# A third gate/value unit begun in the first batch, and batch 5's values loaded behind index 6's keys and queries

## The chip, the cores and the metric

One core of a Trainium2 chip runs the whole program. The metric is the device time of one execution in microseconds (us). Times named by "at" are counted from the start of the profiled span. Batches and banks are counted from 0, so batch 5 is the sixth.

## The reference

Attention without a softmax, followed by a gated feed-forward layer over all tokens:

```
attn = relu(q @ k.T / sqrt(64)) ** 2 / 448          # 8 batches, 12 heads, 448 tokens, 64 wide
x    = (attn @ v), heads side by side               # 3584 tokens x 768
out  = (relu(x @ w_gate) * (x @ w_val)) @ w_out     # 768 -> 1536 -> 768, float32
```

Inputs are float32 in memory and are cast to bfloat16 as they are loaded.

## The kernel before

**Work of a batch.** Scores are made in 21 tiles per batch: three quads of heads (two pairs of two) times seven groups of 64 tokens. `tile_of` makes one with four matmuls, each on a quarter of the array; `relu2` reads it out, ScalarE (ACT) through a Relu (L232) and VectorE (DVE) through a square (L233). `values` (L263) makes a quad of attention outputs with 28 matmuls from the tile `vn`, reads them out, and `exchange` (L258) copies them with the two halves of the partitions swapped, for the units below.

**Gate/value units.** `gv_unit` (L302) makes 128 columns of the hidden layer for one batch: 12 steps of four matmuls on the weights `gv`, into two neighbouring banks of PSUM, then `g_sb` (ACT, L320, reads the first bank) and the product into `hT` (DVE, L321, reads the second). A batch has 12 units. The two banks come from a taker made by `rotation`:

```
sc_first, sc_later, acc = rotation((0, 2, 4)), rotation((0, 2)), rotation((6, 4))
```

Scores and values after the first batch take from `sc_later`, units from `acc`. A take happens when a unit's first step runs. Two units of batch 0 have banks of their own, 4 and 2 (BEGUN_IN, L583): they are begun in `first_batch` (L609) with the four steps that need no exchange. Weight chunk c, loaded by `load_gv(c)`, serves units 2c and 2c+1.

**Order.** It is written out by hand. In iteration b (1 to 6) the loop at L760 runs the units of batch b-1 on TensorE and puts events between their steps: scores and values of the next batches, spread by `paced` (L739), and single events at (unit, step), such as loads. `step` and `turned` (L717 to L726) place the four pieces by which a later batch's keys and queries are turned: `regroup` (L176) on DVE copies them into `kr` or `qr`, and `transpose_grouped` (L183) turns them by DMA transposes issued on SP's queue into `kqT`. Every engine runs its instructions in the order of the program.

**Output stages.** After iterations 2, 4 and 6, `out_pair` (L355) multiplies two batches' hidden layers by `w_out`, in a Strassen form of seven products over four tiles of tokens. Its banks are fixed: P = (6, 7, 0, 1) and Q = (2, 3, 4, 5) for the four tiles. It opens with P's first tile and ends with the adds (L399) of Q's last two. The next iteration's first unit follows, or, after iteration 6, `gv_pair` with fixed banks of its own.

**Loads.** All of them are issued on POOL's queue by `dma_in` (L115). `hold(b)` (L687) puts two tiny copies on POOL that read the last of batch b's turned keys and queries, so POOL issues nothing behind them before those have landed. From batch 2 on all natural keys and queries share one pair of tiles, `kn` and `qn`; values have two tiles in turn. In iteration 4 the values of batch 5 are loaded at unit 0, step 4, and `hold(5)` with the load of index 6 comes at unit 5, step 4. The pieces for batch 5 stand at units 2 and 3, those for batch 6 at units 9 and 10. The first values of batch 5 are made at unit 11, step 5 (L778).

Of the kernel before, what the change touches and what calls it, by code (L numbers as in the profile page):

```python
# [16 lines left out]
def kernel(  # L17
# [172 lines left out]
    def rotation(numbers):  # L190

        turn = [0]

        def take():
            n = numbers[turn[0] % len(numbers)]
            turn[0] += 1
            return banks[:, n:n + 2, :]
        return take
# [52 lines left out]
    def value_passes(b, qd, ps, i0, i1):  # L251

        attn, v_sb = attn_of(b, qd), v_b[b % NB]
        for i in range(i0, i1):
            mm4([ps[:, r, :S] for r in range(2)], lambda r, c: v_sb[:, 2 * qd + c, i, :],
                lambda r, c: attn[:, 2 * i + c, :], i == 0, i == NC - 1)

    def exchange(b, qd):  # L258
        x0, x1 = (x_of[b][e][qd] for e in range(2))
        for (_, p), (_, other) in zip(HALVES, HALVES[::-1]):  # L260
            pin(nc.vector.tensor_copy(x1[p], x0[other]))  # L261
# [40 lines left out]
    def gv_unit(b, mf, order, take):  # L302

        hT = hT_of[b - b % 2]
        c0 = CHUNK_OF[mf]
        w = gv_sb[c0]
        f = mf * 128 - CHUNKS[c0][0]
        col = (b % 2) * S
        o = []

        def step(n, e, hp):
            if n == 0:
                ps = take()
                o.extend(ps[:, r, :S] for r in range(2))
            x = x_of[b][e][hp // 2]
            mm4(o, lambda r, c: w[:, 2 * pair_of(b, hp) + (r ^ e), f + c * 64:f + c * 64 + 64], lambda r, c: x[:, hp % 2, :],
                n == 0, n == H - 1)
            if n == H - 1:
                g_sb = gpool.tile([128, S], BF16, name="g_sb")
                pin(nc.scalar.activation(g_sb, o[0], AF.Relu, scale=float(out_scale)))  # L320
                pin(nc.vector.tensor_tensor(hT[:, mf, col:col + S], o[1], g_sb, ALU.mult))  # L321
        return [lambda n=n, e=e, hp=hp: step(n, e, hp) for n, (e, hp) in enumerate(order)]
# [257 lines left out]
    STRAIGHT = [(e, hp) for e in range(2) for hp in range(HP)]  # L580

    BEGUN = [(e, 2 * qd + c) for qds in (range(0, 2), range(2, 3)) for e in range(2) for qd in qds for c in range(2)]
    BEGUN_IN = (4, 2)  # L583

    def gv_units(b):
        b0 = b - b % 2
        if b == b0:
            hT_of[b0] = hpool.tile([128, KF, 2 * S], BF16, name="hT")
        return [gv_unit(b, mf, BEGUN, rotation((BEGUN_IN[mf],))) if b == 0 and mf < 2 else
                gv_unit(b, mf, BEGUN if mf == 0 else STRAIGHT, acc) for mf in range(KF)]  # L590


# [16 lines left out]
    def first_batch(units):  # L609


        def passes(u, n):
            for _ in range(n):
                units[u].pop(0)()

        def bank(n):
            return banks[:, n, :]

        def tile(n, at=None):
            todo.append(tile_of(0, n, sc_first() if at is None else banks[:, at:at + 2, :]))  # L620

        todo = []

        def scored():
            relu2(*todo.pop(0))

        def second_by_dve():
            src, dst = todo.pop(1)
            r = rpool.tile([128, 2, S], BF16, name="r_sb")
            pin(nc.vector.tensor_scalar(r, src, 0.0, None, ALU.max))  # L630
            scored()
            pin(nc.vector.tensor_tensor(dst, r, r, ALU.mult))

        idle_matmuls(bank(6), 12)
        first_transposes((6, 7, 5, 4))
        idle_matmuls(bank(2), 4)
        tile(0)
        tile(1)
        both = banks[:, 6:8, :]
        for n in range(2, 19):  # L640
            tile(n)
            if n in (3, 5, 7, 9):
                hp = n // 2 + 1
                transposes(0, hp, bank(6 + hp % 2))
            if n in (12, 17):
                value_passes(0, n // 14, both, 0, NC)
            if n == 2:
                second_by_dve()
            elif n > 3:
                scored()  # L650
            if n in (12, 17):
                qd = n // 14
                pin(nc.vector.tensor_copy(x_of[0][0][qd], both[:, :, :S]))  # L653
        tile(19)
        scored()
        passes(0, 4)
        scored()
        tile(20, 0)
        scored()
        value_passes(0, 2, both, 0, 4)  # L660
        scored()
        passes(1, 4)
        value_passes(0, 2, both, 4, NC)
        exchange(0, 0)
        exchange(0, 1)
        pin(nc.scalar.activation(x_of[0][0][2], both[:, :, :S], AF.Copy))
        exchange(0, 2)
        for n in range(4):
            for u in range(2):
                passes(u, 2)  # L670
# [44 lines left out]
        return [(u, min(n, len(units[u]) - 4), e) for (u, n), e in zip(places, events)]  # L715

    def step(units, u, n, k):  # L717
        at = len(units[0]) * u + n + k
        return at // len(units[0]), at % len(units[0])

    def turned(b, units, *at):

# [30 lines left out]

    new_x(0)
    units = gv_units(0)
    first_batch(units)
    load_nat(kn_b[natural(2)], k, 2, 0, H)
    load_gv(5)
    load_nat(qn_b[natural(2)], q, 2, 0, H)
    for b in range(1, B - 1):  # L760
        if b < B - 3:
            new_x(b)
        units = units[2:] if b == 1 else gv_units(b - 1)
        last = len(units) - 1
        if b < B - 4:
            first, behind = {1: (28, 109), 2: (40, 132)}.get(b, (0, 132))
            events = paced(units, first, behind, stream(b, b + 1))
            events.append((last, 8 if b == 1 else 5, values_event(b, NQ - 1)))
        else:
            todo = [e for e in attention if e[:2] <= ENDS[b]]  # L770
            del attention[:len(todo)]
            if b == B - 4:
                begun = flat(kn_b[1], 4, S)
                x_of[b + 1] = [[begun[:, 2 * e:2 * e + 2, :]] for e in range(2)]
                del attention[[e[3] for e in attention].index(NC)]
            events = paced(units, 0, 144 if b == B - 3 else 132, todo)
            if b != B - 3:
                events.append((last, 5, values_event(*((b + 1, 0) if b == B - 4 else (B - 1, NQ - 1)))))  # L778
        if b == 1:
            events += [(1, 2 + 4 * qd, transposes_event(1, qd)) for qd in range(NQ)]  # L780
            events += turned(2, units, (last - 3, 7), (last - 2, 7))
            events += [(last, 2, lambda: (hold(2), load_v(2), load_wo(), load_qk(3)))]
        elif b == 2:
            events += [(1, 1, lambda: load_v(3))]
            events += [(last - 5 + 2 * n, 6, lambda n=n: weight_sums(2 * n)) for n in range(2)]
            events += [(last - 1 + t, 3 + 5 * h, lambda t=t, h=h: regroup(3, t, h)) for t in range(2) for h in range(2)]
            events += [(last, 10, lambda: [transpose_grouped(3, t, h) for t in range(2) for h in range(2)])]
        elif b == 3:
            events += [(2, 1, lambda: (hold_unit(2, 1), hold(3), load_qk(4), load_v(4)))]
            events += turned(4, units, (6, 1), (7, 1)) + [(8, 4, lambda: (hold(4), load_qk(5)))]  # L790
        elif b == 4:
            events += [(0, 4, lambda: load_v(5))]
            events += turned(5, units, (2, 1), (3, 1)) + [(5, 4, lambda: (hold(5), load_qk(6)))]
            events += turned(6, units, (last - 2, 6), (last - 1, 6))
        elif b == 5:
            events += [(2, 1, lambda: (hold_unit(4, 1), load_v(6), hold(6), load_qk(7)))]
            events += turned(7, units, (last - 4, 6), (last - 3, 6))
            later = [xpool.tile([128, HP, S], BF16, name=f"x{n}") for n in range(2)]
            x_of[b] = [x_of[b][e] + quads(later[e])[1:] for e in range(2)]
            x_of[B - 2] = [quads(t)[:1] for t in later]  # L800
        elif b == 6:
            events += [(3, 1, lambda: (hold(7), load_v(7)))]
            new = [xpool.tile([128, HP, S], BF16, name=f"x{n}") for n in range(2)]
            x_of[b] = [x_of[b][e] + quads(new[e])[1:] for e in range(2)]
            x_of[B - 1] = [quads(flat(t, HP, S)) for t in (kr, qr)]
        spread(units, events)
        if b == 2:
            out_pair(0, flat(kn_b[1], KH, S), [lambda: weight_sums(1), lambda: weight_sums(3)])
        elif b == 4:
            out_pair(2, flat(v_b[0], KH, S))  # L810
# [48 lines left out]
```

## Time and profile before

| | us |
|---|---|
| median of three runs | 404.04 |
| the three runs | 404.0, 404.04, 683.68 |
| profiled execution | 403.59 |
| its span, first to last instruction | 401.7 |
| TensorE busy in the span | 390.3 |
| VectorE, ScalarE, GpSimd busy | 303.0, 243.6, 96.5 |

The granted clock of TensorE is 1.000 in the mean. A line of the order of time reads: start, us, engine, source line, operation, written tile <- read tiles, shape, count, and in brackets the engine's idle time before it and what ended it. A line of the waits reads: who waited for whom, us in total, times, the longest. Nearly all matmuls carry L72, a helper's line, so they are told apart by their tiles: `ps<-x,gv` is a unit, `ps<-kqT` a score tile, `ps<-attn,vn` values, `ps<-wo,hT` an output stage, `ps<-blank` idle work at the opening. "PE" is TensorE; "PEld" its weight loads; "SPq" SP's queue.

### The profile page before, as it was taken

The page shows a single profiled execution, that of the slowest core. Times are in us where ns is not written, and L with a number is a line of the kernel's source. Part 1 is how long each engine was busy: PE and PEld are TensorE (multiplying, and loading weights), DVE is VectorE, ACT ScalarE, POOL GpSimd, SP SyncE. Part 2 cuts the span into 40 slices and gives each one's busy share as a digit, 9 for nine tenths or more (in the row PEclk, how much of TensorE's full clock was granted, in tenths as well). Part 3 has the DMA queues.
Part 4 walks back from the last instruction along what each step waited for, and adds up shares of the span by engine and source line. Part 5 has one row for each costly group of instructions (what it writes and reads, how often), then busy time and mean ns, then how long its engine had stood idle before and what let it go on. Part 6 is the DMA issues. An engine that isn't in the chain of part 4 may idle for free.

```text
span 401.7 us, 16575 instructions
## 1 busy us (share of the span) xinstructions
PE 390.3 (97%) x7376; PEld 288.7 (72%) x7376; DVE 303.0 (75%) x530; ACT 243.6 (61%) x358; POOL 96.5 (24%) x168
## 2 busy tenths in 40 slices
PE   8799999999999999999899999999999999999995
PEld 4466779978776666698577666988887766777664
DVE  5975896599944696787691478988889969997922
ACT  4962994787334776988533588899883234344231
POOL 8933301710213600503031360020003230000223
PEclk9999999999999999999999999999999999999999
DMA  9999997999936894997963588760002350000035
GB/s 149 175 196 197 197 190 94 161 205 181 127 91 170 106 164 82 156 149 87 161 116 81 160 107 104 124 86 5 3 2 51 77 154 3 2 3 3 20 89 170
DMA packets 90872, 44.17 MB, mean 110 GB/s; under 512 B 55424, under 2 KB 89792, under 8 KB 90800
## 3 DMA queue, kind: packets, MB, share of 16 engines
q0 software_dynamic: 51264, 28.83, 50.5%
q1 hardware_dynamic: 39104, 13.99, 19.7%
q8 instruction: 57, 0.93, 1.0%
q10 hardware_dynamic: 432, 0.30, 0.3%
q14 instruction: 15, 0.12, 0.1%
HBM read 47.19 MB, written 11.01 MB: 145 GB/s over the span
## 4 chain that ended last, share of the span: by engine, by line
PE 89%; DVE 4%; DMA 3%; ACT 1%; POOL 1%; issue 1%; POOLq 0%; ACTq 0%; DVEq 0%
PE ps L72 88%; DMA qn<-in_q_dram 3%; DVE attn L233 2%; ACT r_sb L232 1%; PE ps L208 1%; POOL qn L116 1%; POOL kn L116 1%; DVE kqT L209 1%; DVE hT L321 0%; DVE x L653 0%; DVE kr L180 0%; DVE x L261 0%; DVE attn L399 0%; POOL ident L112 0%; ACT g_sb L320 0%
## 5 line engine op out<-in xcount | busy, mean ns | idle before, releaser
L72 PE MATMUL ps<-x,gv 64*64 64x448 bf16 x3408 | 198.8, 349 | 1.7 <-DVE hT L321 1.2
L72 PEld LDWEIGHTS <-gv 64*64 64x64 bf16 x4032 | 147.6, 107 | 47.1 <-issue 4.2
L232 ACT ACTIVATE r_sb<-ps 128x896 bf16<-128x896 f32 x167 | 149.0, 933 | 17.2 <-PE ps L72 14.7
L233 DVE TENSOR_TENSOR attn<-r_sb 128x896 bf16<-128x896 bf16 x167 | 101.8, 622 | 28.6 <-ACT r_sb L232 21.8
L409 POOL DMA_DIRECT2D out_dram<-attn x63 | 33.1, 531 | 170.5 <-DVE attn L399 135.2
L72 PEld LDWEIGHTS <-hT 128*64 128x64 bf16 x1056 | 55.8, 110 | 21.0 <-issue 1.4
L72 PE MATMUL ps<-kqT 64*64 64x448 bf16 x672 | 66.7, 351 | 2.8 <-ACT r_sb L232 2.6
L395 ACT ACTIVATE attn<-ps 128x384 f32<-128x384 f32 (+1 forms) x64 | 28.8, 450 | 64.3 <-PE ps L72 63.3
L72 PE MATMUL ps<-wo,hT 128*64 128x384 bf16 (+1 forms) x720 | 54.3, 306 | 0.0
L321 DVE TENSOR_TENSOR hT<-ps,g_sb 128x448 bf16<-128x448 f32 x72 | 44.5, 619 | 8.9 <-ACT g_sb L320 8.2
L320 ACT ACTIVATE g_sb<-ps 128x448 bf16<-128x448 f32 x72 | 39.2, 546 | 17.9 <-PE ps L72 17.6
L399 DVE TENSOR_TENSOR attn<-ps,attn 128x384 f32<-128x384 f32 (+1 forms) x48 | 22.8, 503 | 33.0 <-ACT attn L395 18.4
L72 PEld LDWEIGHTS <-vn 64*64 64x64 bf16 (+1 forms) x888 | 35.5, 107 | 12.4 <-issue 2.3
L72 PE MATMUL ps<-attn,vn 64*64 64x448 bf16 x672 | 37.6, 350 | 0.8 <-DVE attn L233 0.8
L72 PEld LDWEIGHTS <-kqT 64*64 64x64 bf16 x672 | 26.8, 106 | 13.6 <-issue 5.2
L528 ACT ACTIVATE kqT<-ps 128x896 f32<-128x896 f32 x18 | 16.5, 918 | 25.0 <-PE ps L72 25.0
L116 POOL DMA_DIRECT2D vn<-in_v_dram x36 | 23.9, 685 | 16.6 <-PE ps L72 5.8
L72 PE MATMUL ps<-o_ring,hT 128*64 128x384 bf16 (+1 forms) x336 | 26.0, 306 | 0.0
L532 DVE TENSOR_TENSOR kqT<-ps,kqT 128x896 f32<-128x896 f32 x18 | 19.5, 1085 | 5.9 <-PE ps L72 4.2
L690 POOL COPY flag<-kqT 128x1 bf16<-128x1 bf16 x12 | 2.2, 196 | 89.6 <-DMA kqT<-kr 66.8
L261 DVE COPY x<-x 64x896 bf16<-64x896 bf16 x34 | 13.7, 402 | 2.2 <-ACT g_sb L320 0.5
L116 POOL DMA_DIRECT2D qn<-in_q_dram x20 | 14.8, 765 | 1.4 <-POOLq L843 0.8
(101 smaller groups left out, 288.6 us busy)
## 6 DMA issues: line engine op xcount, KB each, us to landing
out_dram<-attn POOLq DMA_DIRECT2D x48, 96.0 KB, 2.3
out_dram<-attn SPq DMA_DIRECT2D x48, 96.0 KB, 2.5
kn<-in_k_dram POOLq DMA_DIRECT2D x7, 384.0 KB, 7.1
qn<-in_q_dram POOLq DMA_DIRECT2D x7, 384.0 KB, 9.5
vn<-in_v_dram POOLq DMA_DIRECT2D x14, 192.0 KB, 8.9
gv<-in_moe_w_gate_dram POOLq DMA_DIRECT2D x6, 384.0 KB, 11.6
gv<-in_moe_w_val_dram POOLq DMA_DIRECT2D x6, 384.0 KB, 11.8
wo<-in_moe_w_out_dram POOLq DMA_DIRECT2D x2, 1152.0 KB, 13.5
```

Of the source, the lines that this page charges most:

```text
L72: pin(nc.tensor.matmul(o, lhsT=l, rhs=r, start=start, stop=stop, skip_group_check=True))
L116: pin(nc.gpsimd.dma_start(out=o, in_=i))
L232: pin(nc.scalar.activation(r, src, AF.Relu))
L233: pin(nc.vector.tensor_tensor(dst, r, r, ALU.mult))
L261: pin(nc.vector.tensor_copy(x1[p], x0[other]))
L320: pin(nc.scalar.activation(g_sb, o[0], AF.Relu, scale=float(out_scale)))
L321: pin(nc.vector.tensor_tensor(hT[:, mf, col:col + S], o[1], g_sb, ALU.mult))
L395: pin(nc.scalar.activation(out_of(t, r, c), bank(P, t), AF.Copy))
L399: pin(nc.vector.tensor_tensor(o, bank(Q, t), o, ALU.add))
L409: pin(engines[c].dma_start(out=rows[:, c0:c1, :], in_=src))
L528: pin(nc.scalar.activation(held(n, j), both(PQ[n][0]), AF.Copy))
L532: pin(nc.vector.tensor_tensor(k, both(PQ[n][1]), k, ALU.add))
```

## The change

Unit 2 of batch 0 gets banks 0 and 1 of its own, runs its first four steps in `first_batch` after the value passes of the last quad and ahead of the exchanges, and no longer takes from `acc`. One take of `sc_later` is thrown away after `first_batch`. `step` uses the length of the last unit in place of the first, and iteration 1 places its scores four steps earlier in a list that is four steps shorter. The load of batch 5's values moves from unit 0, step 4 of iteration 4 to behind the load of index 6's keys and queries at unit 5, step 4.

```
-    BEGUN_IN = (4, 2)
+    BEGUN_IN = (4, 2, 0)
...
-        return [gv_unit(b, mf, BEGUN, rotation((BEGUN_IN[mf],))) if b == 0 and mf < 2 else
+        return [gv_unit(b, mf, BEGUN, rotation((BEGUN_IN[mf],))) if b == 0 and mf < len(BEGUN_IN) else
                 gv_unit(b, mf, BEGUN if mf == 0 else STRAIGHT, acc) for mf in range(KF)]
...
         passes(1, 4)
         value_passes(0, 2, both, 4, NC)
+        passes(2, 4)
         exchange(0, 0)
         exchange(0, 1)
...
     def step(units, u, n, k):
-        at = len(units[0]) * u + n + k
-        return at // len(units[0]), at % len(units[0])
+        at = len(units[-1]) * u + n + k
+        return at // len(units[-1]), at % len(units[-1])
...
     first_batch(units)
+    sc_later()
     load_nat(kn_b[natural(2)], k, 2, 0, H)
...
-            first, behind = {1: (28, 109), 2: (40, 132)}.get(b, (0, 132))
+            first, behind = {1: (24, 105), 2: (40, 132)}.get(b, (0, 132))
...
         elif b == 4:
-            events += [(0, 4, lambda: load_v(5))]
-            events += turned(5, units, (2, 1), (3, 1)) + [(5, 4, lambda: (hold(5), load_qk(6)))]
+            events += turned(5, units, (2, 1), (3, 1)) + [(5, 4, lambda: (hold(5), load_qk(6), load_v(5)))]
```

## The prediction

> **What bounds the kernel now.** I read the page first, then TensorE's list of waits, then the order of time on each engine around the three places that the change touches: the end of the first batch (20 to 36 us), iteration b=4 (160 to 201 us) and both ends of the output stages.
>
> ```profile
> PE 390.3 (97%) x7376; PEld 288.7 (72%) x7376; DVE 303.0 (75%) x530; ACT 243.6 (61%) x358; POOL 96.5 (24%) x168
> PE ps L72 <- ACT r_sb L232: 3.0, 7, 0.6
> PE ps L72 <- DVE hT L321: 1.2, 1, 1.2
> PE ps L72 <- DVE attn L233: 0.8, 1, 0.8
> ```
>
> TensorE is busy for 390.3 of 401.7 us, so only 11.4 us can be won, 2.8%, and part of that is the start and the last stores. Whatever makes TensorE wait is paid in full, since no slack follows. Two idle stretches matter. The larger is at the end of b=4, where both the 1.2 and the 0.8 us lie:
>
> ```profile
> 185.94 0.19 POOL L690 COPY flag<-kqT 128x1 bf16<-128x1 bf16 x1 [5.16 <-DMA kqT<-qr]
> 186.46 1.50 POOL L116 DMA_DIRECT2D kn<-in_k_dram  x2 [0.33 <-DVE hT L321]
> 193.93 0.56 DVE L180 COPY kr<-kn 128x1536 bf16<-128x1536 bf16 x1 [2.10 <-issue]
> 196.08 1.13 PE L72 MATMUL ps<-x,gv 64*64 64x448 bf16 x18 [1.17 <-DVE hT L321]
> 196.87 1.48 PE L72 MATMUL ps<-attn,vn 64*64 64x448 bf16 x24
> 199.11 0.38 PE L72 MATMUL ps<-attn,vn 64*64 64x448 bf16 x4 [0.76 <-DVE attn L233]
> ```
>
> POOL holds the sixth index's keys until batch 5's transposes have landed (185.94); the keys land at 187.19 + 6.7 = 193.9; VectorE, in order, stands at its regroup for 2.10 us (then 0.86 us for the queries at 197.96), and the hT and attn products behind it are late for TensorE. The line at 196.87 is the pass that needs batch 5's values.
>
> The smaller is in the first batch, where TensorE waits for the exchange:
>
> ```profile
> 25.37 0.98 PE L72 MATMUL ps<-attn,vn 64*64 64x448 bf16 x12
> 26.46 6.36 PE L72 MATMUL ps<-x,gv 64*64 64x448 bf16 x120
> 25.94 2.57 DVE L261 COPY x<-x 64x896 bf16<-64x896 bf16 x6
> ```
>
> At these tiles a new matmul starts every 47.5 ns (16 take 0.76 us from start to start). Twelve from 25.37 are issued by 25.94; two more start at 26.46 and the rest, by the chain, at 26.87. So 0.93 - 0.10 = 0.83 us are idle.
>
> **First batch.** passes(2, 4) puts 16 matmuls, 0.76 us, into that hole. Their weights (chunk 1) land at 14.91 + 10.3 = 25.2, before 25.94. Their banks 0 and 1 were last read by ACT's run of seven scores, 19.31 + 5.89 = 25.2. Both covers are under a microsecond; without them the cost would be the lateness itself. The exchange stays where it is, so all that follows moves up 0.76 us. What is late next is batch 1's transposes, which then come at 32.0 for keys and 32.25 for queries: the last query load was issued at 17.85 and took 14.4, so it lands at 32.25. I give back 0.15. Batch 1's first transposes now use banks 2 and 3 through the extra sc_later(); unit 1's last read of them ends at 30.23 + 1.16 = 31.4, so they are free. The changes of step() and of (24, 105) only keep the old places. Gain 0.6; from both sides, 0.3 (queries later by 0.3) to 0.83.
>
> **The bank order that comes with it.** acc alternates (6, 4). Before, batch 0 takes 10 of it and every later batch 12, so a batch's last unit is always in bank 4, and out_pair, whose first product is in bank 6, follows without a wait. With unit 2 in bank 0, batch 0 takes 9, and from then on the last unit of every batch is in bank 6, the first in bank 4. That changes both ends of out_pair.
>
> ```profile
> 100.96 5.24 PE L72 MATMUL ps<-wo,hT 128*64 128x384 bf16 x68
> 100.89 0.54 ACT L320 ACTIVATE g_sb<-ps 128x448 bf16<-128x448 f32 x1 [0.78 <-PE ps L72]
> 200.84 0.54 ACT L320 ACTIVATE g_sb<-ps 128x448 bf16<-128x448 f32 x1 [0.78 <-PE ps L72]
> 300.77 0.54 ACT L320 ACTIVATE g_sb<-ps 128x448 bf16<-128x448 f32 x1 [0.23 <-PE ps L72]
> 124.64 0.85 DVE L399 TENSOR_TENSOR attn<-ps,attn 128x384 f32<-128x384 f32 x2 [1.89 <-PE ps L72]
> 125.02 0.76 PE L72 MATMUL ps<-x,gv 64*64 64x448 bf16 x12
> ```
>
> At the start, the first product must wait until ACT has read bank 6. TensorE resumed 0.05 us after its releaser at 196.08, so it starts at 101.48 instead of 100.96, at 201.43 instead of 200.74, at 301.36 instead of 300.69: 0.52 + 0.69 + 0.67 = 1.9 us. The second product, in bank 7, waits for the hT product, which ends at 102.38, 202.13 and 302.14, just when it comes (0.92 us after the first): nothing more. At the end, the next batch's first unit opens in banks 4 and 5, which the last two adds still read: to 125.14 and 125.49. Its third matmul starts at 125.54 instead of 125.12: 0.42, and the same after the second out_pair (adds from 224.42, unit at 224.81). After the third comes gv_pair with fixed banks. Sum 1.9 + 0.85 = 2.75 us lost. Ends: 1.0, if a tile's drain already hides half of each, to 3.3, if the hT product comes late for bank 7.
>
> The extra sc_later() also swaps banks 0 and 2 for all later scores and values. Around out_pair these are read out at least 0.5 us before they are needed in either order (values' copy ends at 100.36): 0.
>
> **Values of batch 5.** The four loads leave unit 0 of b=4 (POOL 163.25 to 165.9) and follow the sixth index's keys and queries. The queues: POOL has nothing between, so hold(5) stands at the same place. SP's transposes lose a neighbour:
>
> ```profile
> 168.56 7.84 SPq L188 DMA_TRANSPOSE kqT<-kr  x4
> 176.91 7.66 SPq L188 DMA_TRANSPOSE kqT<-qr  x4
> 250.28 6.07 SPq L188 DMA_TRANSPOSE kqT<-kr  x4
> 256.44 6.01 SPq L188 DMA_TRANSPOSE kqT<-qr  x4
> ```
>
> From first transpose to POOL's flag, batch 5 takes 17.4 us with loads landing until 176.5. Batch 7 takes 13.7 with none beside it (263.97), batch 4 takes 15.0 (144.81 to 159.78) with loads until 148.05. With the values gone, loads run until 171.05, 2.5 us of overlap against 8, 0 and 3.2: about 15.3, between batch 4 and the line to batch 5, as its query pieces come 2.6 us apart. The gate opens 2.1 us earlier, the key load is issued at 184.4, the keys land at 191.8, just when VectorE arrives (193.93 - 2.10). The 2.10 us wait goes.
>
> What is late next is the values themselves. Batch 5's own loads had the same order with transposes beside them from the ninth microsecond: first issue 160.29, third value load 164.54 + 10.5 = 175.0, fourth 165.2 + 11.3 = 176.5, so +14.7 and +16.2. From 184.4 that is 199.1 and 200.6; batch 4's own (132.90; 146.4 and 148.05) give 197.9 and 199.5. Nearest is batch 5's pattern, where transposes overlap as here; I take 198.6 and 200.1. Unstalled, TensorE reaches the pass at 195.8, waits 2.8 us, does 16 matmuls to 199.4, waits for the fourth load, and finishes at 200.1 + 0.57 = 200.7. Before, it finished at 199.29. So +1.4 us: the 1.93 us of waits go, about 3.3 come. VectorE's read-out, the exchange and unit 11 queue behind, already in the 1.4. Ends: -1.9, all of the old wait gone and the values in time, to +3.5, the gate no earlier.
>
> **Sum.** -0.6 + 2.75 + 1.4 = +3.5 us. The profiled execution ran 403.59 us (span 401.7 and 1.9 around it); the shown median is 404.04, 0.45 above. 403.59 + 3.5 = 407.1 us, 0.8% slower, within the 2% (8.1 us) that a measurement can tell from no change.
>
> **Rivals.** *The gate opens early enough: not slower.* If the transposes without a neighbour run at batch 7's 13.7 us or better, with issue back to back, the gate opens by 181.5, the values land at 194 to 197, and TensorE hardly stops: -0.6 + 2.75 - 1.9 = +0.25, 403.8; with half of the bank waits hidden, 402.5. It decides once the gate is before 181.5. For it: batch 5's chain is the slowest of all; against: query pieces reach SP only at 171.7 and 174.2. Chance 0.2.
>
> *The bank waits are hidden.* If ACT's read overlaps the change of tile shape, only -0.6 + 1.4 + 0.9 = +1.7, 405.3. For it: 0.27 us already lie between the last gate/value matmul's issue and the first output one at 100.96. Against: the same kind of wait is paid in full at 196.08. Chance 0.15.
>
> *A slow restart.* The opening 24 matmuls on blank data run 4.69 us, 0.195 each; eight of the same kind at 7.01 take 0.92, 0.115 each. If TensorE restarts like that after the values' wait, 4.69 us of work loses 1.9 more: 409.0; beside a late gate, 411. Against: after 1.17 us of idle at 196.08 it went on at full pace; the new wait is 2.8. The granted clock in the profile's rows is 1.00 throughout, the opening included, so those rows don't decide it. [...] Chance 0.1.
>
> **How the numbers follow.** Forecast 0.55, gate 0.2, hidden bank waits 0.15, slow restart 0.1. The range runs from 402.8 (most of the gate case) to 409.5 (late gate without, or restart with, the cold pace). Faster by over 2% would need 8 of 11.4 idle us: 0.02. Slower by over 2% needs restart, late gate and full bank waits together: 0.04. Within: 0.94.
>
> **What would show it.** Right: batch 5's POOL flag near 184; no 2.10 us before the regroup at 191.8; TensorE waiting for the values' load near 196; new waits of 0.5 to 0.7 us on g_sb ahead of each output stage and 0.4 on the adds after two; first transposes 0.6 us earlier. Wrong: a flag before 181.5, no waits at the bank changes, or a stop for chunk 1 or queries in the first batch.

## The result, and the profile after

The changed kernel takes 405.36 us (median of seven runs, 404.95 to 411.81), the kernel before 404.0 (seven runs). The ratio is 1.0051, 95% interval 1.003 to 1.0072, so 2.1 us slower, 1.2 to 2.9. It leaves out runs that lie more than 1.5% above the fastest of their kernel, here 411.81 and 683.68; the first of these will matter below. The profiled execution of the changed kernel has a span of 403.2 us against 401.7, with a granted clock of 1.00.

TensorE's list of waits in the changed kernel (waited for: total, times, longest) has new entries and has lost the two of 1.2 and 0.8 us:

```profile
PE ps L72 <- ACT g_sb L320: 1.5, 3, 0.6
PE ps L72 <- DVE x L267: 0.9, 1, 0.9
PE ps L72 <- DMA vn<-in_v_dram: 0.6, 1, 0.6
PE ps L72 <- DVE hT L321: 0.4, 1, 0.4
PE ps L72 <- DVE attn L399: 0.3, 2, 0.2
```

TensorE's order of time in the changed kernel, at the places that the prediction named (start, duration, and in brackets the idle time before):

```profile
25.11 0.98 PE L72 MATMUL ps<-attn,vn 64*64 64x448 bf16 x12
25.89 5.99 PE L72 MATMUL ps<-x,gv 64*64 64x448 bf16 x120
31.81 0.41 PE L208 MATMUL ps<-ident,kn 128*64 128x128 bf16 x8
38.54 0.38 PE L72 MATMUL ps<-kqT 64*64 64x448 bf16 x4 [0.41 <-DVE hT L321]
100.66 7.03 PE L72 MATMUL ps<-wo,hT 128*64 128x384 bf16 x96 [0.46 <-ACT g_sb L320]
124.94 1.05 PE L72 MATMUL ps<-x,gv 64*64 64x448 bf16 x12 [0.15 <-DVE attn L399]
173.97 0.38 PE L72 MATMUL ps<-kqT 64*64 64x448 bf16 x2 [0.87 <-DVE x L267]
197.53 1.81 PE L72 MATMUL ps<-attn,vn 64*64 64x448 bf16 x26 [0.61 <-DMA vn<-in_v_dram]
201.13 7.03 PE L72 MATMUL ps<-wo,hT 128*64 128x384 bf16 x96 [0.46 <-ACT g_sb L320]
225.41 0.86 PE L72 MATMUL ps<-x,gv 64*64 64x448 bf16 x8 [0.15 <-DVE attn L399]
302.25 7.03 PE L72 MATMUL ps<-wo,hT 128*64 128x384 bf16 x96 [0.61 <-ACT g_sb L320]
```

The hole at 26 us is filled. All three output stages now open with a wait on `g_sb`, and two batches open with a wait on the adds. At the end of b=4 the regroup's waits are gone and the pass waits for the values' load. The kernel before opened its second and third output stage without a bracket (the prediction shows the first):

```profile
200.74 7.03 PE L72 MATMUL ps<-wo,hT 128*64 128x384 bf16 x96
300.69 7.03 PE L72 MATMUL ps<-wo,hT 128*64 128x384 bf16 x96
```

To see where 1.5 us come from, take the same instruction in both traces and the difference (after less before), step by step. Negative is won.

| stretch, by its last instruction | after | before | step, us |
|---|---|---|---|
| opening, value pass | 25.11 | 25.37 | -0.26 |
| early steps, first transposes of batch 1 | 31.81 | 32.75 | -0.68 |
| first score of batch 1 | 38.54 | 39.15 | +0.33 |
| last values of batch 2 | 97.20 | 98.03 | -0.22 |
| first output stage starts | 100.66 | 100.96 | +0.53 |
| first score behind it | 125.65 | 125.61 | +0.34 |
| a score behind batch 5's queries | 174.95 | 173.85 | +1.06 |
| batch 5's first values done | 198.99 | 199.29 | -1.40 |
| second output stage starts | 201.13 | 200.74 | +0.69 |
| first score behind it | 225.93 | 225.21 | +0.33 |
| batch 7's last values start | 298.78 | 297.89 | +0.17 |
| third output stage starts | 302.25 | 300.69 | +0.67 |

The bank order makes 0.53 + 0.34 + 0.69 + 0.33 + 0.67 = +2.56, the early steps -0.68 + 0.33 = -0.35, the moved load +1.06 - 1.40 = -0.34, and the rest, which I put down to no edit, -0.31.

On POOL and VectorE in the changed kernel, the two lines that set the end of b=4, and the one behind the +1.06; the fourth line is that last one in the kernel before:

```profile
182.42 0.22 POOL L691 COPY flag<-kqT 128x1 bf16<-128x1 bf16 x1 [4.83 <-DMA kqT<-qr]
192.90 0.56 DVE L180 COPY kr<-kn 128x1536 bf16<-128x1536 bf16 x1
172.29 0.56 DVE L180 COPY qr<-qn 128x1536 bf16<-128x1536 bf16 x1 [1.50 <-issue]
171.11 0.56 DVE L180 COPY qr<-qn 128x1536 bf16<-128x1536 bf16 x1 [0.53 <-issue]
```

The gate opens at 182.42, not 185.94, and the keys' regroup finds its keys without a wait (no bracket). But VectorE stands 1.50 us for batch 5's own queries, where it stood 0.53 us before, and behind it the values' read-out (L267) keeps TensorE for 0.87 us.

### The profile page after: what moved, and what is told of

Read it like the earlier page. It is cut to its first block, busy times and chain, and to the rows that moved or that the text cites. A ratio compares the mean times of both kernels' runs of the same rounds, so it can differ in the third digit from the quotient of the medians.

```text
span 403.2 us, 16573 instructions
## 1 busy us (share of the span) xinstructions
PE 389.7 (97%) x7376; PEld 309.9 (77%) x7376; DVE 303.1 (75%) x530; ACT 243.4 (60%) x358; POOL 96.8 (24%) x168
## 4 chain that ended last, share of the span: by engine, by line
PE 83%; DMA 6%; DVE 4%; POOL 2%; issue 2%; ACT 2%; SPq 0%; POOLq 0%; ACTq 0%
PE ps L72 82%; DMA qn<-in_q_dram 3%; DMA vn<-in_v_dram 3%; DVE attn L233 2%; ACT r_sb L232 1%; PE ps L208 1%; POOL qn L116 1%; ACT g_sb L320 1%; POOL kn L116 1%; DMA kqT<-qr 1%; DVE kqT L209 1%; POOL vn L116 0%; DVE attn L399 0%; DVE x L267 0%; DVE r_sb L630 0%
## 5 line engine op out<-in xcount | busy, mean ns | idle before, releaser
L72 PE MATMUL ps<-x,gv 64*64 64x448 bf16 x3408 | 201.2, 350 | 0.7 <-ACT r_sb L232 0.3
L72 PEld LDWEIGHTS <-gv 64*64 64x64 bf16 x4032 | 164.6, 107 | 37.3 <-issue 2.2
L232 ACT ACTIVATE r_sb<-ps 128x896 bf16<-128x896 f32 x167 | 148.9, 933 | 20.6 <-PE ps L72 17.5
L72 PE MATMUL ps<-kqT 64*64 64x448 bf16 x672 | 78.5, 351 | 4.1 <-ACT r_sb L232 2.6
L72 PEld LDWEIGHTS <-hT 128*64 128x64 bf16 x1056 | 65.1, 110 | 13.6 <-issue 2.9
L72 PEld LDWEIGHTS <-vn 64*64 64x64 bf16 (+1 forms) x888 | 38.1, 107 | 10.8 <-DMA vn<-in_v_dram 1.6
L72 PEld LDWEIGHTS <-kqT 64*64 64x64 bf16 x672 | 35.6, 107 | 13.4 <-issue 6.3
L72 PE MATMUL ps<-attn,vn 64*64 64x448 bf16 x672 | 39.2, 350 | 0.7 <-DMA vn<-in_v_dram 0.6
L261 DVE COPY x<-x 64x896 bf16<-64x896 bf16 x34 | 13.6, 401 | 2.2 <-ACT g_sb L320 0.5
```

Source lines behind the costliest of these rows:

```text
L72: pin(nc.tensor.matmul(o, lhsT=l, rhs=r, start=start, stop=stop, skip_group_check=True))
L232: pin(nc.scalar.activation(r, src, AF.Relu))
```

## The experiments

Theory: the bank order costs 2.6 us, the early steps win 0.3 to 0.7, and the moved load trades a wait on the regroup for one on the values. Rival for the first: those waits only take the place of others. Each ratio below is against runs of the kernel before on the same chip, in the same group of runs; the three groups ran on different chips, so medians are compared within a group only.

**First group: the parts.**

acc_back, the whole change with the bank order put back:

```
     sc_later()
+    acc()
```

> The whole change, with one further take of acc thrown away after the first batch, so that every batch ends in bank 4 again. Theory (the bank order costs what the new waits show, 0.53 + 0.69 + 0.67 at the starts of the output stages and 0.34 + 0.33 at two ends): no wait on g_sb ahead of the output stages, none on the adds behind them, span 403.2 - 2.6 = 400.6 us, 1.1 us under the span before. Rival (those waits only move a loss that would come elsewhere): the waits go, but less than 1 us is won, span over 402.2.

Measured: median 407.49 (402.57 to 409.08), ratio 1.0074, 1.0032 to 1.0116; span 404.9, clock 0.995. All five bank waits were gone, and it was slower than the kernel before by 3.0 us, where 1.1 less was expected. By its span alone the rival would have it; the two lines on the values below show where the time went. TensorE in acc_back at the end of b=4:

```profile
194.58 1.13 PE L72 MATMUL ps<-x,gv 64*64 64x448 bf16 x18 [1.11 <-DVE hT L321]
196.91 0.38 PE L72 MATMUL ps<-attn,vn 64*64 64x448 bf16 x2 [1.20 <-DMA vn<-in_v_dram]
199.49 2.73 PE L72 MATMUL ps<-attn,vn 64*64 64x448 bf16 x26 [2.20 <-DMA vn<-in_v_dram]
201.65 2.36 PE L72 MATMUL ps<-x,gv 64*64 64x448 bf16 x28
203.94 2.30 PE L72 MATMUL ps<-wo,hT 128*64 128x384 bf16 x26
```

Without the waits in the first output stage TensorE is earlier, while the gate opened at 182.93, 0.5 later than in the changed kernel, since the transposes took 15.7 us; so the values are later still for it. Their third load landed 11.1 us after its issue (9.7 in the changed kernel's profile). And the pass itself is slow: 26 matmuls start over 2.16 us, where the pace before is 47.5 ns each, 1.24 us. The table by stretch of acc_back shows why (stretch, length, busy time and count of the five engines, granted clock, DMA share, GB/s):

```profile
194.00:198.00 4.00, 1.51 (x20) 0.67 (x19) 3.64 (x7) 0.12 (x1) 0.00 (x0) 1.00 1.46 183
198.00:199.50 1.50, 0.01 (x3) 0.01 (x3) 0.06 (x1) 0.00 (x0) 0.00 (x0) 1.00 1.50 111
199.50:201.00 1.50, 1.50 (x20) 0.66 (x24) 0.00 (x0) 0.00 (x0) 0.00 (x0) 0.54 1.30 125
201.00:203.00 2.00, 2.00 (x28) 1.05 (x25) 0.64 (x2) 0.55 (x1) 0.00 (x0) 0.50 1.12 222
203.00:205.00 2.00, 2.00 (x32) 1.11 (x26) 1.30 (x4) 0.54 (x1) 0.00 (x0) 0.99 0.84 191
```

The clock is halved from about 199.6 to 203.0 (0.54 and 0.50 in the rows). My estimate of the loss, half of these 3.4 us, is 1.7 us. This is the slow restart that the prediction had as its last rival.

values_only, the kernel before with the load moved alone:

```
-            events += [(0, 4, lambda: load_v(5))]
-            ... (5, 4, lambda: (hold(5), load_qk(6)))
+            ... (5, 4, lambda: (hold(5), load_qk(6), load_v(5)))
```

> The kernel before, with only the load of batch 5's values moved. Theory (the load that is last in a run of loads is caught behind the transposes' packets, and without the values behind them that is now the query load): the queries of batch 5 land 1 to 1.5 us later after their issue than the 8.5 us of before, VectorE stands 1.5 us at the regroup near 172, TensorE loses about 1 us there and wins 1.4 at the values: span 401.7 - 0.3 = 401.4. Rival (that landing was late by chance, or by where the bank order had moved it): the queries land after 8.5 us, no wait near 173, span 400.3.

Measured: ratio 1.0009, 0.9973 to 1.0045; 401.62 to 408.45; span 402.0, above both. The gate opened at 182.30. Batch 5's queries landed 9.3 us after their issue, VectorE stood 1.08 us for them and TensorE lost 0.61 at 173.50: the way of the theory, but each less than it had. And the pass waited 1.15 and 0.49 us for the values. So the move alone is worth nothing that can be measured, and its six runs lie further apart than the eleven of the kernel before (402.09 to 405.4).

bank_order_only, the kernel before with unit 2 in banks 0 and 1 and the extra take of sc_later, nothing begun early, the load in its old place:

```
-    BEGUN_IN = (4, 2)
+    BEGUN_IN = (4, 2, 0)
...
+    sc_later()
```

> The kernel before, with unit 2 in banks 0 and 1 and the extra take of sc_later, but none of unit 2's steps ahead of the exchange and the values loaded where they were: the bank order alone. Theory: 2.6 us slower, span 404.3, with the five waits of 0.5 to 0.7 and 0.3. Rival (hidden): span under 402.7.

Measured: ratio 1.0067, 1.0036 to 1.0098, 2.7 us of 403.16 (1.5 to 4.0); span 404.3, as the theory had it. Its waits are those of the changed kernel:

```profile
101.21 7.03 PE L72 MATMUL ps<-wo,hT 128*64 128x384 bf16 x96 [0.46 <-ACT g_sb L320]
125.49 1.05 PE L72 MATMUL ps<-x,gv 64*64 64x448 bf16 x12 [0.15 <-DVE attn L399]
202.24 7.03 PE L72 MATMUL ps<-wo,hT 128*64 128x384 bf16 x96 [0.62 <-ACT g_sb L320]
226.52 0.86 PE L72 MATMUL ps<-x,gv 64*64 64x448 bf16 x8 [0.15 <-DVE attn L399]
303.36 6.87 PE L72 MATMUL ps<-wo,hT 128*64 128x384 bf16 x92 [0.61 <-ACT g_sb L320]
```

begun_bank_kept, early steps with the bank order put back, the load in its old place (acc_back with the last edit undone):

> The kernel before, with unit 2 begun ahead of the exchange and a further take of acc thrown away, so that the bank order of later batches is as before; the values loaded where they were. Theory (the four steps fill the wait for the exchange): 0.3 to 0.7 us faster, first transposes 0.7 us earlier against the passes ahead of them, span 401.0 to 401.4. Rival (queries or weights of the first loads take the gain back): no change, 401.7.

Measured: ratio 1.0007, 0.9971 to 1.0042; 402.0 to 406.13; span 400.2. The profile is 1.5 us better, but it had no wait at the end of b=4 either, since its gate opened 1.4 us earlier; the runs don't resolve a gain of 0.3 to 0.7.

**Second group: why the values are late.**

after_again is the changed kernel without an edit.

> The changed kernel once more, beside the next three. Theory (the time hangs on how late the last two value loads are against a TensorE that waits for them): same waits on g_sb and on the adds within 0.1 us, the wait at the values between 0.5 and 3 us, span 402.5 to 405; where the idle time there stays under 3 us the granted clock stays at 1.00. Rival (the time before the values is fixed by the program): the same wait as in the first profile of it, 1.0 us in all, within 0.2.

Measured: median 410.53, 12 runs from 404.36 to 413.58, eight of them over 410; ratio 1.0108, 1.0068 to 1.0148. The profiled one, 413.58, has the same three waits on `g_sb` (0.46, 0.47, 0.61) and two on the adds (0.15, 0.15), and at the values:

```profile
200.39 0.38 PE L72 MATMUL ps<-attn,vn 64*64 64x448 bf16 x2 [1.17 <-DMA vn<-in_v_dram]
204.65 2.82 PE L72 MATMUL ps<-attn,vn 64*64 64x448 bf16 x26 [3.88 <-DMA vn<-in_v_dram]
```

More than 5 us of idle time, with the third value load 12.1 us after its issue and the clock at 0.50 from 201.4 to 208.2. So the rival is out: the wait is not fixed by the program. Its size changes from execution to execution, beyond the 0.5 to 3 us that I gave it, and the span of 411.8 is far outside the 402.5 to 405 as well.

wait_filled, acc_back with 20 matmuls on blank data ahead of the pass:

```
+        ps = sc_later()
+        idle_matmuls(ps[:, 0, :], 10)
+        values(B - 3, 0, ps)
```

> The whole change with the bank order put back (acc_back), and 20 matmuls on blank data ahead of batch 5's first values, in their bank: 1.9 us of work in a place where TensorE stood idle for 4.6 us in the profile of acc_back, with a granted clock of 0.54 and 0.50 in the 3.5 us after it. Theory (the idle time makes the clock fall, and that loses 1.7 us beside the wait itself): clock 1.00 throughout, the pass's 26 matmuls in 1.3 us where they took 2.2, span 1.5 us under that of acc_back, about 403.4, median under acc_back's 407.5. Rival (the loss is the wait alone): same span as acc_back, or up to 1.9 more where the values are in time.

Measured: median 407.6 (404.95 to 411.85), ratio 1.0102, 1.0067 to 1.0137; span 410.1. Inconclusive: in this execution the third value load took 12.9 us, TensorE still stood idle for 3.7 us behind the filler, and the clock fell all the same (0.86 in 200 to 202, then 0.50). The filler was too short to tell wait and clock apart.

values_halved, acc_back with the first half of the values in the old place:

```
+            events += [(0, 4, lambda: load_v(5, HALVES[0:1]))]
+            ... (5, 4, lambda: (hold(5), load_qk(6), load_v(5, HALVES[1:2])))
```

> The whole change with the bank order put back, and only the second half of batch 5's values moved; the first half stays at unit 0 of iteration 4. Theory (what decides is when the last value load lands, and two loads less in front of it bring it 2 us forward, while the transposes lose 1 us of their 3 us gain): value wait under 2.5 us, no fall of the clock, queries of batch 5 landing within 9 us of their issue, span 401 to 402.5. Rival (the gate goes back to 186 with half of the values beside the transposes): both waits, on the regroup and on the values, span 403 or more.

Measured: median 403.8, ratio 1.0014, 0.999 to 1.0039; span 401.4, clock 1.000. Two loads fewer, value waits of 1.12 and 0.50, no fall of the clock, and a stand of 0.63 us for batch 5's queries: as the theory has it. A regroup wait of 1.24 us is left, so the rival's two waits are both there in small.

gate_on_keys, acc_back with the hold reading batch 5's turned keys alone:

```
+            ... (hold(5, (0,)), load_qk(6), load_v(5))
```

> The whole change with the bank order put back, and the hold ahead of index 6's loads waiting for batch 5's turned keys alone, not its queries. Theory (the gate sets when the values land): the gate opens near 175 to 177, keys, queries and values land by 192, TensorE waits neither for the regroup nor for the values; the query transposes share with those loads and land near 187, where batch 5's first score needs them at about 185, so a new wait of 1 to 3 us there; span 401 to 403. Rival (the gate protects nothing): no wait at the scores, span 399 to 400.5.

Measured: ratio 1.0041, 1.0014 to 1.0068; span 403.4, 0.4 over my range. The gate opened at 175.82, and no wait is left at the regroup or the values. A new one came where the theory put it, at batch 5's first score, and the clock fell there (0.64 and 0.51 for 188 to 192). So the gate does protect the transposes:

```profile
184.72 1.27 PE L72 MATMUL ps<-x,gv 64*64 64x448 bf16 x20
188.66 0.59 PE L72 MATMUL ps<-kqT 64*64 64x448 bf16 x4 [2.67 <-issue]
```

**Third group: take away what the loads meet.** In all four, the pieces that turn index 6 go behind the last unit of b=4, so VectorE has no regroup to stand at and no transposes run while the values land:

```
-            events += turned(6, units, (last - 2, 6), (last - 1, 6))
...
         elif b == 4:
+            for t in range(2):
+                for h in range(2):
+                    regroup(6, t, h)
+                    transpose_grouped(6, t, h)
             out_pair(2, flat(v_b[0], KH, S))
```

after_late_turns is the changed kernel with that edit.

> The changed kernel, with index 6's four pieces (regroup and DMA transposes) put behind the last unit of iteration 4, just ahead of the output stage, so that no transposes run while batch 5's values land and VectorE has no regroup to wait for. Theory (the last value loads are late because their last packets are caught behind the transposes): third and fourth value load land within 10.5 us of their issue, where they took 9.7 to 13.3 beside transposes, the granted clock stays at 1.00 and the slow half of the runs (410 and over in after_again) goes: median under 406, span 402 to 403.5. Rival (the loads are late because the gate opens late): landing 11 to 13 us after issue as before, clock falls in half of the runs, median 408 or more.

Measured: median 408.91 (403.66 to 412.23), ratio 1.0079, 1.0046 to 1.0111; span 406.6. The theory that the transposes hold back the value loads fails here: with none beside them, third and fourth still landed 11.7 and 11.9 us after their issue. In the DMA view the loads' queue moved 0.17 MB in the microsecond from 197, and then 0.04, 0.01, 0.01 and 0.01 until 202: a few last packets, alone. The clock stayed at 1.00 around the pass (idle for 1.38 us by the wait), but the median did not come under 406. The rival's numbers came (11 to 13 us, 408 or more); whether the late gate is the cause stays open.

acc_back_late_turns, the same with the bank order put back:

> The same as after_late_turns, with the bank order put back by one further take of acc. Theory (the five bank waits cost 2.6 us, and acc_back lost that again because it brought TensorE nearer to values that were caught): 1.5 to 2.6 us under after_late_turns, the rest of the 2.6 going into a longer wait at the values; median 402 to 404. Rival (the bank waits cost nothing that is not paid elsewhere): same as after_late_turns.

Measured: median 404.56 (403.15 to 411.3), ratio 1.0025, 1.0004 to 1.0047. By the ratios that is 0.0054 of 403.93, 2.2 us, under after_late_turns, within the 1.5 to 2.6, but the two intervals just overlap, and the median is 0.6 over the 402 to 404. Here the third and fourth value loads took 10.2 and 10.3 us.

begun_late_turns, early steps, bank order put back, load in its old place, late turns:

> Unit 2 begun ahead of the exchange, bank order put back, values loaded where they were before, index 6's pieces late as above. Theory (the wait at the end of iteration 4 came from VectorE standing at the regroup, and it can go without moving the values): no wait on hT or attn near 195, values long there, span 399 to 400, median 1 to 3 us under the kernel before. Rival (VectorE's four copies ahead of the output stage's sums make that stage wait): a new wait in the output stage near 207, no gain.

Measured: median 401.47 (400.43 to 402.95) against 403.93, ratio 0.9950, 0.9929 to 0.9972; span 399.7. It has the lowest median and the narrowest spread of its group, and no new wait in the output stage. TensorE in it goes through the pass and into the output stage without a bracket:

```profile
195.43 1.65 PE L72 MATMUL ps<-attn,vn 64*64 64x448 bf16 x28
198.32 7.03 PE L72 MATMUL ps<-wo,hT 128*64 128x384 bf16 x96
```

before_late_turns, the kernel before with the late turns alone:

> The kernel before with nothing but index 6's pieces late. Theory: the 1.17 and 0.76 us of waits go, span 401.7 - 1.9 = 399.8, median 2 us under the kernel before. Rival as for begun_late_turns: no gain.

Measured: median 402.11, ratio 0.9951, 0.9925 to 0.9977, 2.0 us; span 400.7, where I had 399.8. No wait on hT or attn is left in TensorE's list. So what the moved load aimed at could be won without moving it, and the early steps add nothing that these two runs resolve.

## Why the prediction was right, point by point

The direction, the range and the largest term held; one term had the wrong size and one rival was given too small a chance. That the time fell inside the range is in part luck: on the chip of after_again the same kernel was 4.4 us slower by the ratio, and the median of its 12 runs, 410.53, is above the 409.5 at which the range ends.

**First batch, -0.6.** The steps filled the hole as worked out: -0.68 at the first transposes, weights there in time. Of the 0.15 given back to late queries nothing came in the profile shown; in the runs it is between 0 and 1.49 us (after_again). Instead 0.33 went at batch 1's first score, where TensorE has 0.41 us of idle time. The kernel before has a smaller gap at the same place, and what ends it was not settled. Nor is that idle time fixed: of the seven kernels with the early steps and the bank order put back, begun_bank_kept, wait_filled and acc_back_late_turns have it (0.37 to 0.42), the other four have no bracket there. Net -0.35 in this profile, and no run resolves it.

**The bank order, +2.75.** 2.56 in the profile, and 2.7 by bank_order_only's ratio. The three starts are 0.53, 0.69 and 0.67 against 0.52, 0.69 and 0.67; the two ends 0.34 and 0.33 against 0.42. The rival that these waits are hidden is out, by bank_order_only and, less sharply, by the 2.2 us between the two kernels of the third group.

**Values of batch 5, +1.4.** This is the mis-sized term: -0.34 in the profile. "About 15.3" for batch 5's transposes was 13.6 (168.79 to 182.42), the pace of batch 7, which took 13.7 with no loads beside it; I had taken a value between batch 4 and batch 5. The transposes took 17.4 us with the values' loads beside them, in the kernel before, and 13.6 without, in the changed one. But 13.6 is one execution: in the seven profiles with all values behind the full gate the transposes took 13.2 to 13.6 us four times and 15.6 to 15.9 three times (acc_back, after_again, wait_filled), and in the five with the values in place 15.2 to 17.5. So the 15.3 is near what some executions have, and the result's profile had a short one. Then the third and fourth value loads landed at 197.5 and 198.5 instead of 198.6 and 200.1.

What I had not seen at all is the query load: it landed 9.9 us after its issue instead of 8.5. That it is late because it became the last of its run is argued, not shown: it took 8.5 to 9.9 us in the eight profiles with the values moved and 8.5 to 9.2 in the six others. VectorE stood for it 1.0 to 1.5 us in seven of the eight profiles with the values moved (none in acc_back, whose loads went out 3.7 us earlier), and 0 to 0.85 us in the five with them in place and the one with half of them there.

But one execution was a poor guide for this term. The third value load landed 9.7 to 12.9 us after its issue in the seven profiles with the load moved behind a full gate. The pass waits for the end of that, where the old place left about 20 us of slack (fourth load landed at 176.5, pass at 196.87 in the kernel before). I worked out a point from patterns of single executions and gave the ends +3.5; the profile of after_again lost more than that, with 5.05 us of waits for the old 1.93 and about 1.8 more by the halved clock.

**The slow restart, chance 0.1.** It was there in acc_back, gate_on_keys, after_again and wait_filled. Half of the time at work under the half clock, my estimate of its price, is 1.6 to 1.8 us in three of them and 2.9 in wait_filled, against 1.9. That these are near is luck, since 1.9 came from the length of the opening. The pace of the opening changed where the clock records begin: the trace of the kernel before has no clock record ahead of 6.13 us, so the 1.00 in the rows of the opening stands for no record at all, and in the changed kernel, whose first record is at 4.30, pairs of blank matmuls start every 0.373 us until 4.15 and every 0.189 us from 4.42. Eight of 12 runs of the changed kernel on one chip were above 410 us. The one of them with a trace shows the halved clock; of the others only the mean clock is known, 0.990 to 0.996, against 0.995 to 0.999 in the four runs below. On the chip of the result one run of seven was above 410 (411.81, with 0.990). The weak point was the idle time: I took it to be 2.8 us and the same each time.

**The other rivals.** The gate opened at 182.4, 0.9 us short of the point where I had the values in time, and the rest of that case followed in part. The sum with the measured terms is 2.56 - 0.35 - 0.34 - 0.31 = 1.56 for a span that grew by 1.5.

## What to carry to other kernels

An extra user of a rotation of buffers, or one user fewer, turns the parity of everything after it: follow the rotation to every place with fixed buffers before and behind it, since each meeting of the same bank cost the wait for its read-out here (0.5 to 0.7 us three times and 0.3 twice). A load that moves from a place with slack to just ahead of its use turns the spread of its landing into waiting time (here 9.7 to 12.9 us from issue to landing of the third value load), so look at that spread over several executions, not at one. Where a wait comes from an engine that stands at something not yet needed, moving that work later can win the wait (here the regroup, 2.0 us in all).

## What the runs showed of the hardware

The granted clock of TensorE changed in steps of 3.41 us in these runs. It was halved for one such step in acc_back (199.63 to 203.04) and, by rows of 2 us, in gate_on_keys (3.4 us from about 188.6), and for two in after_again (201.40 to 208.23) and wait_filled (6.8 us from about 201.4). In the kernel before and the changed kernel the first record, at full clock, lasts 116 and 117 steps, to 402.07 and 403.66, just behind the last instruction. With these steps as stretches, three in acc_back and four in after_again (the first busy time is TensorE's, the third number from the end its clock):

```profile
192.81:196.22 3.41, 1.79 (x32) 0.72 (x24) 3.05 (x7) 1.31 (x2) 0.00 (x0) 1.00 1.49 190
196.22:199.63 3.41, 0.52 (x6) 0.25 (x10) 1.84 (x4) 0.00 (x0) 0.00 (x0) 1.00 1.45 141
199.63:203.04 3.41, 3.41 (x40) 1.58 (x38) 0.68 (x2) 0.55 (x1) 0.00 (x0) 0.50 1.19 184
197.99:201.40 3.41, 1.61 (x30) 0.73 (x22) 2.62 (x6) 1.00 (x2) 0.00 (x0) 1.00 1.44 178
201.40:204.82 3.42, 0.17 (x4) 0.17 (x8) 0.09 (x1) 0.00 (x0) 0.00 (x0) 0.50 1.43 100
204.82:208.23 3.41, 3.41 (x40) 1.63 (x40) 0.62 (x1) 0.55 (x1) 0.00 (x0) 0.50 1.26 218
208.23:211.64 3.41, 2.94 (x42) 2.11 (x36) 2.74 (x5) 1.03 (x2) 0.00 (x0) 1.00 0.41 93
```

In the step ahead of the fall TensorE was busy for 15% of the time in acc_back (0.52 of 3.41 us) and 47% in after_again (1.61), and for about a quarter in gate_on_keys and wait_filled, an estimate from their rows of 2 us. A step with 52% (1.79, acc_back from 192.81) was followed by full clock, and so were the least busy steps of the kernel before (2.08 us, 61%, from 395.25) and of the changed kernel (2.06, 60%, from 396.83); the very last step of each, without a matmul, was followed by 0.50. By single waits, 1.49 us in after_again (at 33 us) came without a fall; 2.20 in acc_back, behind waits of 1.11 and 1.20, and 2.67 in gate_on_keys came with one, so the 3 us that I had taken as safe ahead of after_again were too much. What sets the clock was not shown.

The last packets of batch 5's value loads came slowly. The loads' queue moved 0.15 to 0.20 MB per microsecond and then, in the changed kernel, 0.05, 0.01 and under 0.01 from 196 to 199, with transposes beside it (0.11, 0.02 and 0.18 MB); in acc_back_late_turns, with none beside it, 0.08, 0.02 and under 0.01 from 196 to 199; in after_late_turns, alone too, 0.04, 0.01, 0.01 and 0.01 from 198 to 202. What holds these packets was not found.
